# Softmax sums of added exponential tiles, and decodes of value weights dealt out over more groups

## The chip, the cores and the metric

The kernel runs on one core of a Trainium2 chip. The metric is the device time of one execution in microseconds (us). Engines are named as in the profile: PE is TensorE (matmuls; PEld is its weight load), DVE is VectorE, ACT is ScalarE, POOL is GpSimd, SP is SyncE, which issues the DMAs here. PE writes into PSUM, whose banks are handed out by a few pools.

## What is computed

Three stages, all in float32: an attention in which a query sees only the keys whose nearest cluster centroid is the same, and two feed-forward layers (called moe in the names, without routing).

```python
# attention: B=2, H=8, S=768, D=64; 16 centroids per head
mask   = q_assign[:, :, :, None] == k_assign[:, :, None, :]
scores = np.where(mask, (q @ k.T) / sqrt(D), -1e9)
attn   = np.exp(scores - scores.max(-1, keepdims=True))
attn   = attn / (attn.sum(-1, keepdims=True) + 1e-9)
x      = attn @ v                          # as 1536 tokens x 512
# layer 1: d_ff = 2048
h = x @ w_in;   x = (max(h, 0) + alpha * min(h, 0)) @ w_out
# layer 2: d_ff = 1536
xn = x / rms(x) * rms_g
x  = (silu(xn @ w_gate) * (xn @ w_val)) @ w_out2
```

The change touches the row sum `attn.sum(-1)` and the order in which weights of the layers are made ready.

## The kernel before, in words

**Attention.** Heads are taken in pairs, eight pairs in all. A pair has two phases, one for each half of its 768 queries, so there are 16 phases, numbered ph = 0 to 15. A phase has T = 6 key tiles of 128 keys, and every key tile has its own slot: phase ph covers the slots 6 ph to 6 ph + 5. In a slot, for each of the pair's two heads (e), `st_tile` (line 535) puts 128 keys x 384 queries of scores into one of three PSUM banks (two matmuls, L545 and L546), and ACT takes the exponential into a tile `p` of 128 x 2 x 384 (L547). Four such tiles exist, in turn. The maximum of each query has been found ahead, by `max_tile` (line 495): two matmuls into the one bank pair `ps_mx` (L503) and a reduction on DVE (L507), once per slot, nine slots before its use.

After every two key tiles, `pv_tiles` (line 549) runs in an even slot. It multiplies the two tiles with the values (L561, output of 64 partitions for each head) and then forms the row sums: matmuls with a matrix of ones (L566), each into 32 partitions of its own of a second bank `sm`, so that head e and tile y stand at partition 32 (2 e + y). The program's four matmuls of a call are eight records in the trace, since a float32 matmul takes two passes. A phase has three calls, for t0 = 0, 2 and 4, in the slots 6 ph + 2, + 4 and + 6. The first starts the accumulation in `sm`, the last ends it. `out_evac` copies both banks to SBUF, `out_sums` (L580) adds up the four partial sums of a query by a matmul, and `out_recip`, `out_bcast`, `out_mult` and `out_split` divide.

**What else runs in the slots.** Pairs are prepared ahead: cluster assignment of the pair's queries and keys, in small DVE steps, and the split of queries and keys into a high and a low part. The tables at the head of the file (PAIR for pairs 4 to 7) say in which slot, relative to the pair's first, each step stands, and in which order within the slot. `norm` are 14 DVE instructions on 128 x 24 (Newton steps of a reciprocal square root; lines 327 to 340), `hi` is a cast on ACT (L461) into a staging tile (`stage`), `lo` a subtraction on POOL (L467). DMAs on SP carry the staging tiles into the matmul operands (L471, L478 to L480); two staging tiles exist, so a pair's `hi` overwrites what the DMAs of the pair two before read. From slot 71 on, the first two halves of the layers' weights are decoded between the phases' work (EARLY). The pool of the preparation's tiles (`at_pre`) is closed at slot 80.

**Layers.** Weights come as 64-bit words and are decoded into a high and a low float32 half: on DVE (`word`, L784 and L786; `tail`, L789 and L790), with a cast on ACT (L797) and two subtractions and additions on POOL (L794, L795). A weight tile is decoded in two halves. Layer 1 has 8 groups of 256 hidden units, layer 2 has 6 (groups 8 to 13). For each group i and each of three blocks n of 512 tokens, `up(i, n)` makes 24 matmuls into two banks; ACT (L860, L861), DVE (L862), ACT (L869, the high part gh) and POOL (L870, the low part gl) follow for each. `down(i, n)` multiplies g with the output weights into ps_mx (y = 0) and ps_pv (y = 1), 12 matmuls each, and DVE adds each bank pair to x (L914). Layer 2 has a second up product with value weights `wv` (w_val).

**The order of the layers' work** is made by `plan` (line 960). It writes the sequence: up(p), then down of the step before p, so a down usually stands two of these slots behind its own up. At the end of layer 1, down(6, 2) is moved behind down(7, 0), so there up(7, 0), up(7, 1) and down(7, 0) follow each other. Decodes wait in the list `todo`, first in, first out. After the first half (y = 0) of every up or down one of them is placed, unless the slot is marked busy or the list is empty. At the end of the last up of group i, the up weights of group i + 2 are put on the list (two halves, or four with wv), at the end of its last down the down weights. The value weights of groups 8 and 9 (`split_v`) are put on it early: four groups ahead, that is at the ends of groups 4 and 5.

Of the kernel before, what the change touches and what calls it, by code (L numbers as in the profile page):

```python
# [13 lines left out]
ALU = mybir.AluOpType  # L14
# [8 lines left out]
    "load": ((-41, 6.1), (-41, 6.2), (-39, 6.1), (-38, 6.1)),  # L23
    "sq": ((-35, 4), (-34, 4)),
    "ss": ((-34, 5), (-33, 5)),
    "norm": tuple((-32 + n // 5, 5 + (n % 5) / 10) for n in range(14)),
    "hi": ((-32, 4), (-31, 4)),
    "lo": ((-28, 4.5), (-22, 4.5)),
    "sims": ((-30, 2.5), (-29, 1.7)),
# [50 lines left out]
    3: (11, 11, 12, 13, 14, 15),  # L80
}
DIRECT = 4
ASIDE = (1, 2, 3)
WARM = (6, 10, 1, 1, 3)
EARLY = (
# [93 lines left out]
class Attention:  # L179
    def __init__(self, base, core, ops, prep, tc, banks, qt, kt, qn, kn, vn, centroids, x1h, x1l, idf, idr):  # L180
        self.nc = tc.nc
        self.bk = banks
        self.qt, self.kt, self.qn, self.kn, self.vn = qt, kt, qn, kn, vn
        self.x1h, self.x1l, self.idf, self.idr = x1h, x1l, idf, idr
        self.NP, self.T, self.D = qn.shape[0], qn.shape[2], qn.shape[4]
        self.S = self.T * 128
        self.HS = self.S // 2
        self.NH = 2 * self.NP
        self.H, self.C = centroids.shape[:2]
        self.centroids = centroids  # L190
        self.scale = 1.0 / float(self.D) ** 0.5
        S, T, C = self.S, self.T, self.C

        def pool(ctx, name, bufs, **kw):
            return ctx.enter_context(tc.tile_pool(name=name, bufs=bufs, **kw))

        one = pool(core, "at_one", 1)
        self.v_p = pool(core, "at_vn", 2)
        self.p_p = pool(core, "at_p", 4)
        self.o_p = pool(core, "at_o", 2)  # L200
        self.x_p = pool(core, "at_x", 2)
        self.s_p = pool(core, "at_s", 2)
        pool(base, "at_pad", 1, side="right").tile([128, LINE - 8], F32, name="pad")
        stages = pool(base, "at_st0", 1, side="right"), pool(prep, "at_st1", 1, side="right")
        self.stages = [p.tile([128, 4, S], F32R, name=f"stage{i}") for i, p in enumerate(stages)]
        self.pre_p = pool(prep, "at_pre", 1, side="right")
        self.pre_p.tile([128, LINE // 4], F32, name="pad")
        ops = pool(ops, "at_ops", 1)
        self.op1 = [ops.tile([128, 2, S], F32R, name=f"op1_{i}") for i in range(4)]
        self.op2 = [ops.tile([82, 2, S], F32R, name=f"op2_{i}") for i in range(4)]  # L210
        self.cb = one.tile([128, self.H // 2, 2 * C], F32, name="cb")
        self.code = one.tile([128, C], F32, name="code")
        self.ohs = one.tile([128, 1], F32, name="ohs")
        self.rc0 = one.tile([128, 1], F32, name="rc0")
        self.mh = [one.tile([128, T // 2, 64], F32R, name=f"mh{i}") for i in range(2)]
        self.cb0 = one.tile([128, 2 * C], F32, name="cb0")
        self.sel = one.tile([128, LINE], F32, name="sel")[:, :2]
        for n in ("raw", "nat", "norm", "ss", "sims", "simc", "simp", "am", "oh", "oht", "pv", "P", "vnat",
                  "mx", "osb", "ssb", "sums", "rs", "R", "X"):
            setattr(self, n, {})  # L220
# [271 lines left out]
    def halves(self):  # L492
        return [(g, slice(g * self.HS, (g + 1) * self.HS)) for g in range(2)]
# [55 lines left out]
    def pv_tiles(self, u):  # L549


        nc, T = self.nc, self.T
        ph, t0 = divmod(2 * u, T)
        if t0 == 0:
            self.pv[ph] = self.bk.pv()
        ps, sm = self.pv[ph][:, 0, :self.HS], self.pv[ph][:, 1, :self.HS]
        P = [self.P.pop(2 * u + y) for y in range(2)]
        how = dict(start=t0 == 0, stop=t0 == T - 2)
        for y in range(2):
            for e in range(2):  # L560
                nc.tensor.matmul(ps[64 * e:64 * e + 64], lhsT=self.vnat[ph // 2][:, e, t0 + y], rhs=P[y][:, e],  # L561
                                 start=t0 + y == 0, stop=t0 + y == T - 1)
        for e in range(2):
            for y in range(2):
                r = 32 * (2 * e + y)
                nc.tensor.matmul(sm[r:r + 32], lhsT=self.ones[:, 0:32], rhs=P[y][:, e], **how)  # L566

    def out_evac(self, ph):
        nc = self.nc
# [118 lines left out]
class Moe:  # L688
# [271 lines left out]
    def plan(self):  # L960
# [10 lines left out]
        a, b = seq.index((self.down, (n1 - 2, NB - 1))), seq.index((self.down, (n1 - 1, 0)))  # L971
# [3 lines left out]
        tags = lambda i: ["wi", "wv"] if self.groups[i][0] else ["wi"]  # L975
        split_v = (n1, n1 + 1)
        halves = lambda i, ts: [(i, t, x) for t in ts for x in range(2)]
        out, dec, todo = [], [], []
        for i, t in ((1, "wi"), (0, "wo"), (1, "wo")):
            dec += halves(i, [t])  # L980
        pre = len(dec)
# [1 line left out]
        for fn, (i, n) in seq:  # L983
            last = n == NB - 1
            for y in range(2):
# [15 lines left out]
                        else:  # L1001
                            rms_at[self.up, *nxt[1], 1] = (self.rms_mul, n)
                if last and y and fn == self.up:
                    if i + 4 in split_v:
                        todo += halves(i + 4, ["wv"])
                    if i + 2 < NG:
                        todo += halves(i + 2, tags(i + 2)[:1] if i + 2 in split_v else tags(i + 2))
                if last and y and fn == self.down and i + 2 < NG:
                    todo += halves(i + 2, ["wo"])
                busy = (fn == self.down and (i == n1 - 1 or (i, n, y) == (n1 - 2, NB - 1, 1))  # L1010
# [144 lines left out]
```

## Time and profile before

| | us |
|---|---|
| median of three runs | 895.16 (894.52 to 896.11) |
| profiled execution, its own time | 896.74 |
| its span, first to last instruction | 895.0 |
| busy in the span: PE / DVE / POOL / ACT | 861.4 / 586.1 / 393.6 / 326.0 |
| mean granted clock of PE, share of 2.4 GHz | 0.985 |

Times in the profile are counted from the span's start. The attention's main loop runs from about 36 to 312 us, the layers from there to the end. A row of a timeline gives the start, the time, the engine, the line, the operation and its tiles; the bracket at its end is the engine's idle time before it and what ended it. "x8" means that eight instructions of the same kind are merged. Matmuls overlap, so starts of successive ones are closer than their durations.

### The profile page before, as it was taken

Reading aid. Unit: us, or ns where it says so; the run is one execution under the profiler, and the core shown is the slowest. Engines: PE = TensorE matmul, PEld = TensorE weight load, DVE = VectorE, ACT = ScalarE, POOL = GpSimd, SP = SyncE. Lnnn points to the kernel's source line nnn. Section 1 sums busy time; section 2 is a strip of 40 time slices with the busy share of each in tenths; the row PEclk is TensorE's granted clock in tenths of the full one; section 3 lists DMA queues with packets and bytes.
Section 4 is the critical chain, followed back from the end, with each engine's and each line's share of the span. In section 5 each row is a group of like instructions: output and inputs, shape, how many; then the busy total and the mean of one; then the engine's idle time right before and its main releaser. Section 6 shows DMA issues by size and latency. Waiting matters only on the chain.

```text
span 895.0 us, 11602 instructions
## 1 busy us (share of the span) xinstructions
PE 861.4 (96%) x4351; PEld 639.6 (71%) x4351; DVE 586.1 (65%) x906; ACT 326.0 (36%) x623; POOL 393.6 (44%) x349
## 2 busy tenths in 40 slices
PE   6898999999999999999999997999999999999998
PEld 4555565565555688888888875778888888888886
DVE  7765666565467546888778997887565465455422
ACT  4544465564445414333333334342212212222110
POOL 3651121121002516676657777433654554554511
PEclk9798999999999999999999998999999999999999
DMA  7768075265271201122212222000211211211012
GB/s 217 214 186 203 18 187 115 99 147 109 60 191 64 80 1 47 59 83 72 71 48 94 75 90 71 24 24 17 79 59 60 71 63 56 71 63 55 1 47 95
DMA packets 24279, 75.69 MB, mean 85 GB/s; under 512 B 3680, under 2 KB 4896, under 8 KB 24224
## 3 DMA queue, kind: packets, MB, share of 16 engines
q1 hardware_dynamic: 24224, 74.96, 29.1%
q8 instruction: 34, 0.56, 0.3%
q14 instruction: 21, 0.17, 0.1%
HBM read 51.46 MB, written 3.15 MB: 61 GB/s over the span
## 4 chain that ended last, share of the span: by engine, by line
PE 78%; DVE 10%; ACT 5%; issue 3%; POOL 1%; DMA 1%; SPq 1%; ACTq 0%; DVEq 0%
PE ps_st L807 26%; PE ps_mx L807 11%; PE ps_pv L807 10%; PE ps_pv L561 8%; PE ps_pr L807 5%; PE ps_pv L566 4%; PE ps_mx L503 4%; PE ps_st L545 3%; DVE dec_a L786 2%; PE ps_st L546 2%; PE ps_pr L594 2%; DVE x L914 1%; DVE dec_a L784 1%; ACT p L547 1%; ACT op L532 1%
## 5 line engine op out<-in xcount | busy, mean ns | idle before, releaser
L507 DVE TENSOR_REDUCE mx<-ps_mx 128x1 f32<-128x768 f32 x93 | 89.0, 957 | 85.2 <-PE ps_mx L503 84.7
L870 POOL TENSOR_TENSOR gl<-v,gh 128x512 fp32r<-128x512 f32 x68 | 93.7, 1378 | 110.3 <-ACT gh L869 108.5
L547 ACT ACTIVATE p<-ps_st 128x384 f32<-128x384 f32 x192 | 83.3, 496 | 57.7 <-PE ps_st L546 57.0
L611 POOL TENSOR_TENSOR x1l<-X,x1h 128x384 fp32r<-128x384 f32 x15 | 15.1, 1006 | 192.3 <-ACT x1h L608 192.3
L869 ACT CAST gh<-v 128x512 fp32r<-128x512 f32 x68 | 42.2, 621 | 134.4 <-DVE v L866 81.8
L866 DVE TENSOR_TENSOR v<-ps_st,t 128x512 f32<-128x512 f32 x36 | 24.9, 691 | 90.6 <-PE ps_st L807 90.6
L545 PE MATMUL ps_st<-op 128*128 128x384 f32 x192 | 71.4, 372 | 7.2 <-ACT p L547 7.2
L561 PE MATMUL ps_pv<-p,vnat 128*64 128x384 f32 x384 | 74.0, 507 | 0.0
L786 DVE SCALAR_TENSOR_TENSOR dec_a<-raw,dec_a 128x512 uint32<-128x512 uint32 x66 | 69.0, 1046 | 2.3
L862 DVE SCALAR_TENSOR_TENSOR v<-v,alpha,t 128x512 f32<-128x512 f32 x45 | 46.5, 1033 | 36.1 <-ACT v L861 36.1
L807 PE MATMUL ps_st<-x1h,stage 128*128 128x512 f32 x272 | 68.1, 391 | 0.0
L546 PE MATMUL ps_st<-op 82*128 82x384 f32 x192 | 66.1, 344 | 1.5 <-DMA op<-stage 1.5
L914 DVE TENSOR_TENSOR x<-ps_mx,x 128x1024 f32<-128x1024 f32 x36 | 43.8, 1218 | 32.6 <-PE ps_mx L807 32.6
L794 POOL TENSOR_TENSOR dec_a<-dec_a,woh 128x512 f32<-128x512 f32 x28 | 45.5, 1624 | 36.4 <-ACT woh L797 32.1
L503 PE MATMUL ps_mx<-op 80*128 80x384 f32 x186 | 54.7, 376 | 5.4 <-DVE mx L507 5.4
L807 PEld LDWEIGHTS ps_st<-x1h,stage 128*128 128x128 f32 x272 | 50.9, 188 | 11.0
L807 PE MATMUL ps_st<-x1h,wvh 128*128 128x512 f32 x144 | 57.1, 397 | 0.0
L807 PE MATMUL ps_st<-x1h,wvl 128*128 128x512 f32 x144 | 56.7, 394 | 0.0
L503 PEld LDWEIGHTS ps_mx<-op 80*128 80x128 f32 x186 | 31.5, 195 | 34.8 <-issue 15.6
L807 PE MATMUL ps_st<-x1h,wih 128*128 128x512 f32 x132 | 52.7, 399 | 0.1
L807 PE MATMUL ps_st<-x1h,wil 128*128 128x512 f32 x132 | 51.9, 393 | 0.0
L789 DVE TENSOR_SCALAR dec_e<-dec_a 128x512 uint32<-128x512 uint32 x66 | 49.5, 750 | 2.2
(250 smaller groups left out, 1989.3 us busy)
## 6 DMA issues: line engine op xcount, KB each, us to landing
raw<-in_moe_w_out_dram SPq DMA_DIRECT2D x28, 512.0 KB, 3.5
op<-stage SPq DMA_DIRECT2D x32, 384.0 KB, 5.7
raw<-in_moe_w_in_dram SPq DMA_DIRECT2D x15, 512.0 KB, 3.5
raw<-in_moe_w_val_dram SPq DMA_DIRECT2D x12, 512.0 KB, 3.4
raw<-in_moe_w_gate_dram SPq DMA_DIRECT2D x12, 512.0 KB, 3.4
op<-stage SPq DMA_DIRECT2D x16, 288.0 KB, 5.8
nat<-in_qn_dram SPq DMA_DIRECT2D x8, 384.0 KB, 5.1
nat<-in_kn_dram SPq DMA_DIRECT2D x8, 384.0 KB, 5.3
```

Of the source, the lines that this page charges most:

```text
L503: nc.tensor.matmul(ps[:, g, :self.HS], lhsT=o1[0:80, 0, t * 128:(t + 1) * 128], rhs=o1[0:80, 1, sl], start=True, stop=True)
L507: nc.vector.tensor_reduce(out=self.mx[ph][:, k:k + 1], in_=ps[:, :, :self.HS], op=ALU.max, axis=AX.XY)
L545: nc.tensor.matmul(ps, lhsT=o1[:, 1, ks], rhs=o1[:, 0, qs], start=True, stop=False)
L546: nc.tensor.matmul(ps, lhsT=o2[:, 1, ks], rhs=o2[:, 0, qs], start=False, stop=True)
L547: nc.scalar.activation(out=p[:, e], in_=ps, func=AF.Exp, scale=self.scale)
L561: nc.tensor.matmul(ps[64 * e:64 * e + 64], lhsT=self.vnat[ph // 2][:, e, t0 + y], rhs=P[y][:, e], start=t0 + y == 0, stop=t0 + y == T - 1)
L786: v.scalar_tensor_tensor(out=a, in0=top, scalar=0xC0000000, in1=a, op0=ALU.bitwise_and, op1=ALU.bitwise_or)
L789: v.tensor_scalar(out=e, in0=a, scalar1=0xFF800000, scalar2=None, op0=ALU.bitwise_and)
L807: self.nc.tensor.matmul(ps, lhsT=a, rhs=b, start=first and i == 0, stop=last and i == len(terms) - 1)
L862: nc.vector.scalar_tensor_tensor(out=v, in0=v, scalar=self.nalpha[:, a], in1=t, op0=ALU.mult, op1=ALU.add)
L870: nc.gpsimd.tensor_tensor(out=lo, in0=v, in1=f(hi), op=ALU.subtract)
L914: nc.vector.tensor_tensor(out=dst, in0=ps, in1=dst, op=ALU.add)
```

## The change

Three edits.

1. In phases 4 to 12 (`SUMMED`), the calls of `pv_tiles` with t0 = 0 and t0 = 2 issue no matmuls for the sums. Each adds its two exponential tiles on DVE into a tile of its own (`add0`, `add1`, 128 x 2 x 384, in the preparation's pool). The call with t0 = 4 then issues two rounds of the sums' matmuls: one over the two added tiles (it starts the accumulation), one over its own two tiles (it ends it).
2. The 14 `norm` steps of pairs 4 to 7 stand otherwise in the same three slots, -32, -31 and -30 before the pair: 1, 6 and 7 of them in place of 5, 5 and 4.
3. The decodes of the value weights of groups 8 and 9, four halves, are put on the list one at a time, at the ends of the last ups of groups 0, 1, 2 and 3, behind the up weights of group i + 2.

```diff
-    "norm": tuple((-32 + n // 5, 5 + (n % 5) / 10) for n in range(14)),
+    "norm": tuple((t, 5 + n / 100) for n, t in enumerate([-32] + [-31] * 6 + [-30] * 7)),
...
+SUMMED = range(4, 13)
...
+        self.adds = []
...
-        for e in range(2):
-            for y in range(2):
-                r = 32 * (2 * e + y)
-                nc.tensor.matmul(sm[r:r + 32], lhsT=self.ones[:, 0:32], rhs=P[y][:, e], **how)
+        if ph in SUMMED and t0 < T - 2:
+            a = self.pre([128, 2, self.HS], f"add{t0 // 2}")
+            self.adds.append(a)
+            nc.vector.tensor_tensor(out=a, in0=P[0], in1=P[1], op=ALU.add)
+            return
+        rounds = [self.adds, P] if ph in SUMMED else [P]
+        for x, q in enumerate(rounds):
+            if ph in SUMMED:
+                how = dict(start=x == 0, stop=x == 1)
+            for e in range(2):
+                for y in range(2):
+                    r = 32 * (2 * e + y)
+                    nc.tensor.matmul(sm[r:r + 32], lhsT=self.ones[:, 0:32], rhs=q[y][:, e], **how)
+        self.adds = []
...
-        out, dec, todo = [], [], []
+        out, dec, todo, split = [], [], [], [h for i in split_v for h in halves(i, ["wv"])]
...
                 if last and y and fn == self.up:
-                    if i + 4 in split_v:
-                        todo += halves(i + 4, ["wv"])
                     if i + 2 < NG:
                         todo += halves(i + 2, tags(i + 2)[:1] if i + 2 in split_v else tags(i + 2))
+                    todo += split[:1]
+                    split = split[1:]
```

Worked out by hand from this loop, the slots (one up or one down) that carry a decode change as follows. Before: six in a row from up(1, 2) to down(2, 0), then pairs with a free slot between them up to up(4, 0) and down(4, 0), then 14 in a row from down(4, 1) to up(7, 0). After: three from down(1, 0) to up(1, 1), 12 in a row from up(1, 2) to down(3, 0), five from down(3, 1) to down(4, 0), then pairs with a free slot between them up to up(7, 0). From group 8 on, both are the same.

## Rows read from the trace of the kernel before

**Rows 1.** Busy time by stretch: PE, PEld, DVE, ACT, POOL; PEclk; DMA share, GB/s.

```profile
100.00:300.00 200.00, 192.95 (x1311) 118.77 (x1308) 126.30 (x249) 100.27 (x228) 31.48 (x26) 1.00 0.47 117
300.00:540.00 240.00, 239.56 (x1080) 191.74 (x1080) 188.10 (x206) 89.79 (x162) 156.38 (x104) 1.00 0.19 64
```

**Rows 2.** Timeline of PE in slot 26: the call t0 = 0 of phase 4.

```profile
115.90 1.51 PE L561 MATMUL ps_pv<-p,vnat 128*64 128x384 f32 x8
...
116.28 0.14 PEld L561 LDWEIGHTS ps_pv<-p,vnat 128*64 128x64 f32 x2 [0.18 <-issue]
...
117.34 0.16 PEld L566 LDWEIGHTS ps_pv<-p,ones 128*32 128x32 f32 x8 [0.60 <-issue]
...
118.12 0.62 PE L503 MATMUL ps_mx<-op 80*128 80x384 f32 x2
```

**Rows 3.** Lines L467, L786 and L328 on DVE: durations in ns, least, median, greatest.

```profile
L467 DVE TENSOR_TENSOR stage<-raw,stage x2: 949/950/951, 16.1 to 16.9; 128x768 fp32r<-128x768 f32 x2
...
L786 DVE SCALAR_TENSOR_TENSOR dec_a<-raw,dec_a x66: 691/693/1674, 271.4 to 842.4; 128x512 uint32<-128x512 uint32 x66
...
L328 DVE SCALAR_TENSOR_TENSOR n_a<-n_a,n_y x9: 182/182/186, 123.5 to 194.6; 128x24 f32<-128x24 f32 x9
```

**Rows 4.** Timeline of DVE and PE in phase 12, around slots 77 and 78.

```profile
259.75 0.96 DVE L507 TENSOR_REDUCE mx<-ps_mx 128x1 f32<-128x768 f32 x1 [0.93 <-PE ps_mx L503]
...
261.17 0.52 PE L503 MATMUL ps_mx<-op 80*128 80x384 f32 x2
```

**Rows 5.** Timeline of ACT and PE in slot 29 (phase 4) and slot 41 (phase 6).

```profile
124.70 0.84 ACT L461 CAST stage<-raw 128x768 fp32r<-128x768 f32 x1 [3.08 <-DMA vnat<-in_vn_dram]
...
125.44 0.86 ACT L547 ACTIVATE p<-ps_st 128x384 f32<-128x384 f32 x2
...
126.06 0.37 PE L545 MATMUL ps_st<-op 128*128 128x384 f32 x1
...
158.31 0.83 ACT L461 CAST stage<-raw 128x768 fp32r<-128x768 f32 x1 [2.69 <-DMA vnat<-in_vn_dram]
...
160.05 0.34 PE L545 MATMUL ps_st<-op 128*128 128x384 f32 x1
```

**Rows 6.** Timeline of PE at down(7, 0), and one stretch of 2 us there.

```profile
546.97 0.39 PE L807 MATMUL ps_mx<-gh,woh 128*128 128x512 f32 x1
547.19 0.40 PE L807 MATMUL ps_mx<-gh,wol 128*128 128x512 f32 x1
...
552.06 0.80 PE L807 MATMUL ps_mx<-gh,woh 128*128 128x512 f32 x1 [4.46 <-ACT gh L869]
...
556.86 0.40 PE L807 MATMUL ps_pv<-gh,woh 128*128 128x512 f32 x1
...
550.00:552.00 2.00, 0.00 (x0) 0.00 (x0) 1.19 (x1) 0.74 (x3) 1.92 (x2) 0.50 0.56 168
```

**Rows 7.** Timeline within the run of 14 decodes: ACT, PE and DVE.

```profile
482.61 0.60 ACT L860 ACTIVATE t<-ps_st 128x512 f32<-128x512 f32 x1 [0.53 <-PE ps_st L807]
...
525.55 1.07 PE L807 MATMUL ps_st<-x1l,stage 128*128 128x512 f32 x4
...
530.76 0.59 ACT L860 ACTIVATE t<-ps_st 128x512 f32<-128x512 f32 x1
...
532.58 0.50 PE L807 MATMUL ps_pv<-gh,woh 128*128 128x512 f32 x1 [0.43 <-DVE x L914]
...
535.46 0.39 PE L807 MATMUL ps_st<-x1h,wih 128*128 128x512 f32 x1
...
543.48 1.22 DVE L914 TENSOR_TENSOR x<-ps_pv,x 128x1024 f32<-128x1024 f32 x1
```

**Rows 8.** Timeline around up(4, 0): the next matmul behind it on PE, POOL's gl.

```profile
440.91 0.40 PE L807 MATMUL ps_mx<-stage,woh 128*128 128x512 f32 x1
...
446.64 1.28 POOL L870 TENSOR_TENSOR gl<-v,gh 128x512 fp32r<-128x512 f32 x1
```

**Rows 9.** Busy time of one stretch in phase 2, columns as in rows 1.

```profile
82.00:90.00 8.00, 7.38 (x39) 4.31 (x37) 4.92 (x13) 3.04 (x6) 0.00 (x0) 0.57 0.54 194
```

## The prediction

> **What bounds the kernel now.** I read three views in order. First the busy time by stretch [rows 1]: between 100 and 300 us, the attention stage, TensorE (PE) is busy 193 of 200 us, and from 300 to 540 us, the first expert layer, 239.6 of 240. At these places a microsecond is won only by taking work from PE or by removing one of its few waits. Then PE's own instructions in one softmax slot [rows 2], to price the sums of the exponentials. Last the one large hole of PE behind 300 us, 547 to 552 us, with the queues of DVE, ScalarE (ACT) and POOL around it [rows 6]. PE waits there for an activation that DVE computed late. Behind the hole the granted clock is 0.50, its lower level of 1.2 GHz, where it was 1.00 while PE ran without a gap. So the change has two parts on PE's path, and one that only moves small DVE work (the norm steps).
>
> **Part A: sums of exponentials.** A phase has six key tiles, two per call of pv_tiles, and each call ends with one round of eight ones-matmuls (L566). A round costs PE from 117.34 to 118.12, 0.78 us, the start of the next line's matmuls included [rows 2]. In phases 4 to 12 the first two calls lose their round, the third gets a second one (over the two added tiles, ahead of the one over its own pair). So 2 x 0.78 goes and one round comes.
>
> The added round follows another of the same shape. Its nearest rows are the value matmuls just before: eight of them, two key tiles behind each other, take 115.90 to 117.34, 1.44 us or 0.72 per tile, and weight loads (116.28) run inside them. I take 0.72; the bounds are 0.64 (two steps of 0.32, the load of 116.28 and the gap before it) and 0.94 (a full 0.78, and 0.16 for loads that find nothing to hide behind). Net gain of a phase 1.56 - 0.72 = 0.84 us, of nine 7.6 us (bounds 5.6 to 8.3).
>
> The Trainium skill, page "TensorE: Matmul & The Clock Gate", section "Part 3: Packing small matmuls — row/col tiling", says that a weight load overlaps running matmuls only when the row groups differ. Here all loads cover the same 128 rows, so by it the second round would pay its loads in full, and the sum of part A would be 5.6, not 7.6. The trace goes the other way at the loads of 116.28, though those loads are 64 columns wide and the ones in question 32.
>
> **What DVE pays.** 18 additions of 128x768 with both inputs and output in SBUF. DVE did that shape twice, at 0.95 us [rows 3]; the upper bound is what a two-input DVE instruction takes when POOL runs beside it, 0.69 growing to 1.67. POOL is busy 31 of 200 us here [rows 1], so I take 0.95: 17 us of DVE in 150 us, on 126 of 200 busy [rows 1]. DVE has the time. Its order matters more: the addition stands ahead of the next maximum's reduction, and PE has one bank for maxima. In most slots the reduction still ends before PE asks for the bank; a shortened call (0.78 earlier) and the addition (0.95) together shift this by about 1.7 us.
>
> At one phase this does not fit. In phase 12 the first weights' decode shares the slots: before, the reduction of 259.75 ended at 260.7 and PE took the bank at 261.17 [rows 4]. Now PE would come 1.56 earlier, at 259.6, while the reduction comes no sooner: PE waits about 1.1 us, and 0.1 in the slot pair before. I price phase 12 at -1.2. The moved norm steps keep the other additions' slots free: of 14 instructions of 0.18 us [rows 3] four leave a slot with an addition for two without one. I price them at nothing, since DVE's idle time before the reductions covers them there; without it, 4 x 0.18 = 0.7 us in each of four pairs.
>
> **What DMA and ACT set.** In phases 4, 6 and 8 a cast on ACT (L461) overwrites a staging tile that DMAs of the previous pair still read. It starts when they land, at 124.70 after 3.08 us of idle ACT, and exponentials queue behind it (125.44) [rows 5]. The SP queue issues those DMAs back to back from the start of the phase, so their landing does not come earlier by what PE saves inside the phase. The fourth score tile needs the first one's exponential, one of the two that take 0.86: not before 125.9. Before it started at 126.06; PE could now be there 1.56 earlier, and gets only some 0.1 to 0.2. That loses 1.4 in phase 4. In phase 6 (cast 158.31 to 159.14, first exponential done 159.6, fourth tile at 160.05 before) PE is only 0.84 ahead, because the previous phase's longer last call lies behind the DMAs' start: it loses 0.4. Phase 8 has the same pattern, 0.6 at most. The smaller DVE waits of these phases fall into the same gaps. **Part A: 7.6 - 1.2 - 1.4 - 0.4 - 0.6 = 4.0 us**, between 2 and 7.6.
>
> **Part B: the decodes.** Before, four value-weight decodes are queued at groups 4 and 5, so that 14 slots in a row carry one each. DVE falls behind: the scores' first read came at once at 482.61 (ACT waited for PE), but at 530.76 for matmuls that ended at 526.6, eight slots later [rows 7]. So the lag grows 4.1 / 8 = 0.5 us per slot with a decode. Usually down(p) stands two slots behind up(p); at (7, 0) it stands one behind, and the lag becomes PE's wait. The two parts of that hole [rows 6]: 547.19 + 0.23 to 552.06 is 4.6 us of idle, and the 12 matmuls from 552.06 to 556.86 take 4.80 instead of 12 x 0.23 = 2.7 at full clock, 2.1 us. A bank wait of 0.43 at 532.58 comes from the same lag [rows 7]. Removable: 7.1 us.
>
> After, reading the schedule: groups 1 to 3 carry a run of 12 decodes in a row, then a gap, five, and from there two and a gap, up to (7, 0). That last pattern stood at (4, 0) before: the up group ended at 440.9, its last gl was ready at 446.64 + 1.28 = 447.9 [rows 8], 7.0 us later. The down group needs it one slot of 24 matmuls at 0.23 and five matmuls later, 5.5 + 1.1 = 6.6 us. So 0.4 us of wait remains at (7, 0), and the clock holds.
>
> The run of 12 brings its own lag, at its end the same as that of slots 12 and 13 before. There down's second bank was added at 543.48 + 1.2 = 544.7 for a down that ended when the next up began, 535.46: 9.2 us, and two slots later a down asks for that bank after 5.5 and 2.7 more, 8.2 [rows 6, 7]. So 1.0 us of new wait at down(3, 1), and 0.43 at down(3, 0) as at 532.58: 1.5 us, from 0 (the lag starts later) to 4.6 (as much as the hole of before). **Part B: 7.1 - 0.4 - 1.5 = 5.2 us**, between 0.5 and 7.1.
>
> The DMAs of the raw weights move with their decodes, three buffers ahead. Their queue, SP's, issues nothing else in that layer, and the DMA engines are busy 0.19 of it [rows 1], so I price that at nothing; if a load came late, its decode would wait on DVE and add to the same lag.
>
> **Sum.** 4.0 + 5.2 = 9.2 us. The profiled execution took 896.74 us, 895.0 in its span and 1.7 around it: 887.5. The median of the three runs shown is 895.16, 1.58 below it: **886.0 us**.
>
> **Rivals.**
> *All covers hold.* PE never waits for the additions, the cast or the run of 12: 7.6 + 7.1 - 0.4 = 14.3, so 880.9. For it: DVE is idle a third of the attention stage. Against it: the casts at 124.70 and 158.31, which PE hardly trails today. 20%.
> *The hole only moves.* The run of 12 stalls PE in group 3 as the run of 14 did: part B gives 0, 891.2. For it: the lag per slot is the same. Against: down stands two slots behind there. 12%.
> *The second round hides nothing.* It pays 0.78 and its loads' 0.16, the upper bound above: 9 x 0.22 = 2.0 us less, 888.0. For it: those loads stand in front of the first round today, after 0.60 of idle loader. Against: the loads at 116.28. 10%.
> *Part A does nothing.* Adding on DVE makes the maxima late in every phase, so that the matmuls saved are waited away: 890.0. 6%.
> *Slower: the clock.* From 82 to 90 us, where PE had waited shortly before (and idles for another 0.6 of the 8), the granted clock averaged 0.57 [rows 9], 0.43 x 8 = 3.4 us lost. New waits of 1 us stand at five places (phases 4, 6, 8, 12, group 3). If each brought one such fall, 17 us would go: 902.9; from the third fall on the change is slower. Against: most of the waits are shorter than 1 us, and stand alone. 6%.
> The Trainium skill, same page, section "HAM oscillation — how this bites in real kernels", says that gaps between bursts of matmuls bring the lower clock back, each anew; the rows at 80 to 90 us and at 552 us agree.
>
> **How the numbers follow.** The forecast has 46%. The range 880.5 to 891.5 takes in all but the clock rival and the forecast's own outer bounds. A difference under 0.2% (1.8 us) is about what a measurement of this kernel cannot tell from none. Every case but the clock's is faster by more, 0.94 together; I take 0.03 of that for both parts falling short at once: faster 0.91, within 0.03, slower 0.06.
>
> **What would show it.** Right: nine rounds of eight matmuls fewer from L566; 18 new DVE additions near 0.95 us; a summed phase 0.84 us shorter where no cast waits; ACT's cast in phases 4, 6, 8 still on DMA and the next score matmul waiting for an exponential; no hole near (7, 0) and a clock of 1.00 there; a small wait on ps_pv in group 3. Wrong: additions well above 1 us, PE waiting on L507 in every phase, or a low clock between 100 and 550 us.

## The result, and the profile after

| | before | after |
|---|---|---|
| median, runs beside each other (us) | 895.63 (894.52 to 897.06, 4 runs) | 887.08 (882.80 to 888.32, 4 runs) |
| profiled execution, its span (us) | 896.74, 895.0 | 886.97, 885.2 |
| busy PE / DVE / POOL / ACT (us) | 861.4 / 586.1 / 393.6 / 326.0 | 852.6 / 597.8 / 393.8 / 325.9 |
| mean granted clock | 0.985 | 0.988 |

The ratio is 0.9902, 95% interval 0.9875 to 0.9928: 8.6 us faster, against a forecast of 9.2. In the code after, the lines stand 3 further down, and 12 or 13 further behind the added ones: max matmul L506 and reduction L510 (503 and 507 before), scores L548 and L549, exponential L550, value matmul L564, addition L569, sums L578, copy of the sums L586, cast L464, layer matmul L820, addition to x L927.

First the busy time of the profiled execution after, by stretch (columns as in [rows 1]):

```profile
100.00:300.00 200.00, 190.29 (x1264) 120.34 (x1265) 143.35 (x271) 102.25 (x233) 36.01 (x29) 1.00 0.47 117
300.00:540.00 240.00, 238.82 (x1067) 191.47 (x1066) 192.81 (x211) 90.70 (x164) 158.75 (x105) 1.00 0.19 66
540.00:560.00 20.00, 20.00 (x91) 16.23 (x90) 14.02 (x26) 7.26 (x13) 7.37 (x6) 1.00 0.08 27
```

Against [rows 1] DVE has 17 us more in the attention, and the hole of [rows 6] is gone: PE works all 20 us around (7, 0), at clock 1.00. PE is *less* busy in the attention than before: it does less and waits a little more.

Then the lines of the addition and of its sums (durations in ns, least, median, greatest):

```profile
L569 DVE TENSOR_TENSOR add<-p x18: 916/932/948, 118.1 to 253.7; 128x768 f32<-128x768 f32 x18
...
L578 PE MATMUL ps_pv<-add,ones x72: 486/498/510, 128.8 to 259.0; 128*32 128x384 f32 x72
```

18 additions at 0.93 us (0.95 was taken); PE's matmuls fall from 4351 to 4279, the 9 x 8 expected.

**Phase by phase.** The copy of the sums on ACT ends every phase, and its start is in the trace to 0.01 us. From one copy to the next is the length of a phase. Before, phases 4 and 5:

```profile
112.71:130.28 17.57, 16.95 (x119) 10.52 (x120) 12.32 (x32) 10.86 (x24) 2.79 (x2) 1.00 0.90 228
130.28:146.71 16.43, 15.76 (x108) 9.53 (x107) 9.29 (x15) 7.18 (x19) 3.00 (x3) 1.00 0.17 32
```

The same phases after:

```profile
113.54:131.42 17.88, 16.24 (x111) 10.41 (x112) 13.77 (x34) 10.86 (x24) 2.80 (x2) 1.00 0.86 224
131.42:146.84 15.42, 14.76 (x100) 9.45 (x99) 10.81 (x17) 7.18 (x19) 3.00 (x3) 1.00 0.22 46
```

Phase 5 is 1.01 us shorter (16.43 - 15.42), all of it PE work. Phase 4 also lost 0.7 us of PE work, and is 0.31 *longer*: it waits. This table gives the difference for every phase, before minus the kernel named (us); the last six columns are the experiments below.

| phase | after | A alone | old norm | casts +1, +1 | casts +1, +2 | two additions | rounds apart |
|---|---|---|---|---|---|---|---|
| 4 | -0.31 | -0.74 | -2.27 | 0.98 | 0.98 | -1.59 | -2.65 |
| 5 | 1.01 | 1.00 | 1.00 | 0.25 | 1.00 | -0.10 | 0.86 |
| 6 | -0.07 | 0.50 | 0.11 | 0.93 | 0.91 | -1.02 | 0.42 |
| 7 | 0.99 | 0.99 | 0.99 | -1.31 | 1.00 | 0.13 | 0.87 |
| 8 | 0.27 | -0.18 | 0.12 | 0.93 | 0.94 | -0.99 | -0.58 |
| 9 | 0.97 | 0.97 | 0.99 | 0.25 | 0.98 | 0.11 | 0.84 |
| 10 | 0.91 | 0.91 | 0.92 | 0.92 | 0.91 | 0.64 | 0.79 |
| 11 | 0.60 | 0.60 | 0.61 | 0.60 | 0.60 | -0.39 | 0.46 |
| 12 | 0.22 | 0.22 | 0.24 | 0.24 | 0.22 | -3.37 | 0.09 |
| 4 to 12 | 4.59 | 4.27 | 2.71 | 3.79 | 7.54 | -6.58 | 1.10 |

So the 9.8 us between the two spans are: 4.59 in phases 4 to 12; 6.01 from the last copy to the last addition to x, the layers; and -0.83 up to the end of phase 3, where the two kernels differ only in the order of the norm steps of slots 16 to 18. Of this 0.71 stands ahead of the first copy, in the start-up and phase 0, which the change does not touch.

### The profile page after: what moved, and what is told of

The parts are those of the page before. It is cut to its first block, busy times and chain, and to the rows that moved or that the text cites. A ratio compares the mean times of both kernels' runs of the same rounds, so it can differ in the third digit from the quotient of the medians.

```text
span 885.2 us, 11463 instructions
## 1 busy us (share of the span) xinstructions
PE 852.6 (96%) x4279; PEld 637.5 (72%) x4279; DVE 597.8 (68%) x924; ACT 325.9 (37%) x623; POOL 393.8 (44%) x349
## 4 chain that ended last, share of the span: by engine, by line
PE 77%; DVE 11%; ACT 5%; issue 3%; DMA 2%; POOL 1%; SPq 1%; ACTq 0%; DVEq 0%
PE ps_st L820 27%; PE ps_mx L820 11%; PE ps_pv L820 11%; PE ps_pv L564 7%; PE ps_pr L820 5%; PE ps_mx L506 4%; PE ps_pv L578 3%; PE ps_st L548 3%; DVE mx L510 2%; DVE dec_a L799 2%; PE ps_st L549 2%; DVE x L927 2%; ACT p L550 1%; DMA op<-stage 1%; PE ps_pr L607 1%
## 5 line engine op out<-in xcount | busy, mean ns | idle before, releaser
L510 DVE TENSOR_REDUCE mx<-ps_mx 128x1 f32<-128x768 f32 x93 | 88.8, 955 | 67.9 <-PE ps_mx L506 67.7
L550 ACT ACTIVATE p<-ps_st 128x384 f32<-128x384 f32 x192 | 83.3, 496 | 51.6 <-PE ps_st L549 51.0
L548 PE MATMUL ps_st<-op 128*128 128x384 f32 x192 | 71.7, 373 | 9.4 <-ACT p L550 9.4
L564 PE MATMUL ps_pv<-p,vnat 128*64 128x384 f32 x384 | 74.3, 509 | 0.0
L820 PE MATMUL ps_st<-x1h,stage 128*128 128x512 f32 x272 | 68.1, 391 | 0.0
L549 PE MATMUL ps_st<-op 82*128 82x384 f32 x192 | 66.1, 344 | 1.1 <-DMA op<-stage 1.1
L927 DVE TENSOR_TENSOR x<-ps_mx,x 128x1024 f32<-128x1024 f32 x36 | 43.9, 1218 | 32.4 <-PE ps_mx L820 32.4
L506 PE MATMUL ps_mx<-op 80*128 80x384 f32 x186 | 55.0, 377 | 5.9 <-DVE mx L510 5.8
L820 PEld LDWEIGHTS ps_st<-x1h,stage 128*128 128x128 f32 x272 | 50.9, 188 | 11.0
L820 PE MATMUL ps_st<-x1h,wvh 128*128 128x512 f32 x144 | 57.1, 396 | 0.0
L506 PEld LDWEIGHTS ps_mx<-op 80*128 80x128 f32 x186 | 31.1, 194 | 35.8 <-DVE mx L510 12.0
L820 PE MATMUL ps_st<-x1h,wvl 128*128 128x512 f32 x144 | 56.7, 394 | 0.0
L820 PE MATMUL ps_st<-x1h,wih 128*128 128x512 f32 x132 | 52.5, 398 | 0.0
L820 PE MATMUL ps_st<-x1h,wil 128*128 128x512 f32 x132 | 51.9, 393 | 0.0
L548 PEld LDWEIGHTS ps_st<-op 128*128 128x128 f32 x192 | 37.2, 194 | 20.4 <-ACT p L550 19.4
```

The costliest lines, as they stand in the source:

```text
L506: nc.tensor.matmul(ps[:, g, :self.HS], lhsT=o1[0:80, 0, t * 128:(t + 1) * 128], rhs=o1[0:80, 1, sl], start=True, stop=True)
L510: nc.vector.tensor_reduce(out=self.mx[ph][:, k:k + 1], in_=ps[:, :, :self.HS], op=ALU.max, axis=AX.XY)
L548: nc.tensor.matmul(ps, lhsT=o1[:, 1, ks], rhs=o1[:, 0, qs], start=True, stop=False)
L549: nc.tensor.matmul(ps, lhsT=o2[:, 1, ks], rhs=o2[:, 0, qs], start=False, stop=True)
L550: nc.scalar.activation(out=p[:, e], in_=ps, func=AF.Exp, scale=self.scale)
L820: self.nc.tensor.matmul(ps, lhsT=a, rhs=b, start=first and i == 0, stop=last and i == len(terms) - 1)
```

## The experiments

Ten kernels ran. Where a time differs by less than 1%, the phases say more than the medians.

**1. Part A alone: the decodes as before.**

```diff
-        out, dec, todo, split = [], [], [], [h for i in split_v for h in halves(i, ["wv"])]
+        out, dec, todo = [], [], []
...
+                    if i + 4 in split_v:
+                        todo += halves(i + 4, ["wv"])
...
-                    todo += split[:1]
-                    split = split[1:]
```

> Part A without part B: the added sums and the moved norm steps, with the decodes queued as before. Theory (the two parts are independent; A is worth 4.6 us between the ends of phases 3 and 12, B is the hole at (7, 0)): the copy of the sums at the end of phase 12 stands 4.6 us closer to that of phase 3 than before, within 0.4; the hole of 4.6 us near (7, 0) and the half clock behind it are still there; time 4.6 below the kernel before, ratio 0.995. Rival (A and B share something, for example DVE's lag is carried from one to the other): the hole shrinks or grows by over 1 us, and the time is below 0.993 or above 0.997.

891.38 us, ratio 0.9954 (0.9934 to 0.9974). 4.27 in phases 4 to 12, 0.09 in the layers. Its waits of PE from 312 to 560 us (us in total, times, longest):

```profile
PE ps_mx L820 <- ACT gh L882: 4.5, 1, 4.5
PE ps_pv L820 <- DVE x L927: 0.4, 1, 0.4
```

The hole is there in full. The theory holds.

**2. Part B alone: the kernel before with the decodes dealt out** (the reverse edit in the kernel before).

> Part B without part A: the decodes dealt out over four groups, sums as before. Theory: no hole near (7, 0), clock 1.00 there, waits of about 1.1 us on ps_pv in group 3, 6.0 us gained between the start of layer 1 and its end, nothing in the attention stage; ratio 0.9933. Rival (part A brought some of the gain in the layer): 4 us or less, ratio above 0.995.

889.92 us, ratio 0.9932 (0.9907 to 0.9958). No phase from 4 to 12 differs by more than 0.08; the layers gain 6.15, where the seven traces with these layers give 6.01 to 6.17. The hole is gone, and ps_pv waits 1.1 us, in 2 waits. The two parts add up, within their intervals: 0.46% and 0.68% against 0.98% together. What fell short of the theory's "nothing in the attention stage" is phase 2, 2.94 us shorter with the same instructions (see the clock below).

**3. The norm steps back at 5, 5 and 4.**

```diff
-    "norm": tuple((t, 5 + n / 100) for n, t in enumerate([-32] + [-31] * 6 + [-30] * 7)),
+    "norm": tuple((-32 + n // 5, 5 + (n % 5) / 10) for n in range(14)),
```

> The changed kernel with the norm steps of pairs 4 to 7 back at 5, 5 and 4 a slot. Theory (DVE's idle time before the reductions covers them): every phase as in the changed kernel within 0.2 us, the same time within 0.5 us. Rival (an addition and five norm steps in one slot make the maximum late): up to 0.7 us in each of four pairs, 2.8 us slower, with waits of the maxima's matmuls on DVE's reduction in phases 1, 3, 5 and 7 after the pair's start three ahead.

885.75 us, ratio 0.9889 (0.9861 to 0.9917), not to be told from the changed kernel. Every phase of the table but 4, 6 and 8 agrees within 0.02. Phase 4 lost 2.27, but not to a reduction: PE waited 1.38 there for an exponential behind the cast, and the clock then fell (0.65 on average from 125 to 128 us). So no gain of the moved norm steps shows in the time. But in phase 8 the rival's wait is there. With the steps back, five of them stand between the addition and the reduction, which ends at 192.80:

```profile
190.03 0.94 DVE L569 TENSOR_TENSOR add<-p 128x768 f32<-128x768 f32 x1
...
191.85 0.95 DVE L510 TENSOR_REDUCE mx<-ps_mx 128x1 f32<-128x768 f32 x1
...
192.85 0.62 PE L506 MATMUL ps_mx<-op 80*128 80x384 f32 x2 [0.35 <-DVE mx L510]
```

In the changed kernel one step stands there, and the reduction ends 0.88 before PE comes, which had waited for the cast:

```profile
189.88 0.94 DVE L569 TENSOR_TENSOR add<-p 128x768 f32<-128x768 f32 x1
...
190.83 0.95 DVE L510 TENSOR_REDUCE mx<-ps_mx 128x1 f32<-128x768 f32 x1
...
192.66 0.52 PE L506 MATMUL ps_mx<-op 80*128 80x384 f32 x2
```

So it is mostly the wait for the cast that covers the old order in phases 4, 6 and 8, and not DVE's idle time. The order moves the reduction's end by 0.87 (2.77 or 1.90 behind the start of the addition). Without the cast's wait (experiment 5) the margin there is only 0.22, so by estimate the old order would cost about 0.65 in each of these phases; no run shows it.

**4. The hi casts of pairs 4 to 7 one slot later.** What phase 4 waits for, in the changed kernel, on ACT:

```profile
125.20 0.83 ACT L464 CAST stage<-raw 128x768 fp32r<-128x768 f32 x1 [3.54 <-DMA vnat<-in_vn_dram]
125.94 0.86 ACT L550 ACTIVATE p<-ps_st 128x384 f32<-128x384 f32 x2
```

and on PE:

```profile
126.47 0.44 PE L548 MATMUL ps_st<-op 128*128 128x384 f32 x1 [1.01 <-ACT p L550]
```

This is the chain of the prediction: DMA, cast, exponential, fourth score tile. The bracket names a load of v, but that is inferred. On SP's queue the last DMA that reads the staging tile stands just ahead of it:

```profile
119.19 1.90 SPq L483 DMA_DIRECT2D op<-stage  x1
121.19 1.38 SPq L361 DMA_DIRECT2D vnat<-in_vn_dram  x1
```

The first landed 5.8 us after its start, at 125.0, just before the cast; the load landed after 4.5 us, at 125.7, when the cast was running. If this chain is the cause, moving the cast alone must free all three phases.

```diff
-    "hi": ((-32, 4), (-31, 4)),
+    "hi": ((-31, 4), (-30, 4)),
```

> The changed kernel with both hi casts of pairs 4 to 7 one slot (about 5 us) later. Theory (the cast that waits for DMAs holds ACT, and the exponentials behind it hold the score tiles): the cast finds its tile free, phases 4, 6 and 8 come to the 0.97 us gained by the undisturbed phases, from -0.31, -0.07 and 0.27: 3.0 us faster than the changed kernel, ratio to the kernel before 0.987. Rival 1 (the maxima's bank behind the additions holds PE in those phases as well): under 1 us of it comes. Rival 2 (the casts now delay another exponential, or the operands' DMAs start later and arrive late): no gain, or up to 1 us slower.

885.49 us, ratio 0.9886 (0.9862 to 0.9911). Phases 4, 6 and 8 gain 0.98, 0.93 and 0.93, as the theory said to 0.05. But phases 5, 7 and 9 (and 3, by 0.54) lost, as the first half of rival 2 said (the casts delay another exponential). ACT around the start of phase 7:

```profile
161.10 0.49 ACT L400 ACTIVATE simc<-ps_pr 128x384 f32<-128x384 f32 x1 [2.39 <-PE ps_pr L395]
161.49 0.47 ACT L586 COPY ssb<-ps_pv 128x384 f32<-128x384 f32 x1
161.85 0.50 ACT L586 COPY osb<-ps_pv 128x384 f32<-128x384 f32 x1
162.22 0.86 ACT L464 CAST stage<-raw 128x768 fp32r<-128x768 f32 x1
162.95 0.53 ACT L621 CAST x1h<-X 128x384 fp32r<-128x384 f32 x1
163.36 1.71 ACT L550 ACTIVATE p<-ps_st 128x384 f32<-128x384 f32 x4
```

The second cast now stands in the slot in which ACT already makes four other copies, and the exponentials come after all five. PE, and then its clock (last number but two of the stretch 165 to 168):

```profile
163.93 0.45 PE L548 MATMUL ps_st<-op 128*128 128x384 f32 x1 [0.95 <-ACT p L550]
...
165.00:168.00 3.00, 3.00 (x13) 1.16 (x12) 2.59 (x6) 0.08 (x1) 1.33 (x1) 0.56 0.00 0
```

In phases 5 and 9 the wait cost 0.7 to 0.8; in phase 7 a clock of 0.56, near the lower level of 1.2 GHz, followed, and 2.3 us went.

**5. The second cast one slot further**, past the copies.

```diff
-    "hi": ((-32, 4), (-31, 4)),
+    "hi": ((-31, 4), (-29, 4)),
```

> The changed kernel with the hi casts of pairs 4 to 7 one and two slots later, so that none stands in the slot in which ACT also copies the sums out. Theory (the landing of the previous pairs' DMAs sets phases 4, 6 and 8, and the copy's slot was what cost phases 5, 7 and 9 in the kernel with both casts one slot later): phases 4, 6 and 8 gain 0.95 as there, phases 5, 7 and 9 gain 0.97 again as in the changed kernel; together about 3 us over the changed kernel, at 884. Rival (any later place of the cast meets some exponential): phases 5, 7 and 9 stay at 0.25 or less, and the sum is 1 us or less.

880.03 us, ratio 0.9840 (0.9816 to 0.9863). All six phases at 0.91 to 1.00; phases 4 to 12 give 7.54 instead of 4.59, the 3 us expected. The cast finds its tile free, and the exponentials do not wait (ACT in phase 4):

```profile
121.41 0.58 ACT L444 ACTIVATE oht<-ps_pr,ohs 128x384 fp32r<-128x384 f32 x1
121.88 0.84 ACT L464 CAST stage<-raw 128x768 fp32r<-128x768 f32 x1
122.60 0.89 ACT L550 ACTIVATE p<-ps_st 128x384 f32<-128x384 f32 x2
```

So the DMAs' landing, through the cast on ACT, took 3 us of what the additions saved.

**6. The dealing at groups 0, 2, 3 and 4.**

```diff
-                    todo += split[:1]
-                    split = split[1:]
+                    if i in (0, 2, 3, 4):
+                        todo += split[:1]
+                        split = split[1:]
```

> The changed kernel with the value weights' halves put on the list at the last ups of groups 0, 2, 3 and 4, so that the longest run of slots with a decode is 6 instead of 12 (runs of 3, 6, 5, 5, 5, then 2, 2, 2). Theory (DVE's lag grows 0.5 us per slot of a run and costs PE from about the tenth on): no wait on ps_pv in group 3, none elsewhere, no hole at (7, 0); 1.1 us faster than the changed kernel in the first layer. Rival 1 (a run of 5 with one gap carries its lag over): the waits only move to groups 4 to 6, same time. Rival 2 (with the fourth half nearer to the end, DVE is late at (7, 0)): part of the hole of 4.6 us and of the low clock is back, 1 to 5 us slower.

882.29 us, ratio 0.9872 (0.9836 to 0.9908). No wait of PE is listed from 312 to 560 us. From 400 to 440 us, in this kernel:

```profile
400.00:440.00 40.00, 40.00 (x175) 32.55 (x174) 36.27 (x39) 15.06 (x27) 30.10 (x21) 1.00 0.25 80
```

and in the changed one:

```profile
400.00:440.00 40.00, 38.87 (x167) 31.02 (x166) 36.74 (x41) 14.98 (x27) 30.03 (x21) 1.00 0.24 82
```

DVE is about as busy; it only never has 12 decodes in a row. The layers gain 8.21 over the kernel before, 2.0 to 2.2 more than with the change's order, where the theory took 1.1 from the waits as listed. The list is too low. One of the two waits, PE in the changed kernel:

```profile
429.10 0.63 PE L820 MATMUL ps_mx<-gl,woh 128*128 128x512 f32 x2
430.49 0.50 PE L820 MATMUL ps_pv<-gh,woh 128*128 128x512 f32 x1 [0.77 <-DVE x L927]
430.83 0.40 PE L820 MATMUL ps_pv<-gh,wol 128*128 128x512 f32 x1
```

Matmuls start 0.23 apart when nothing is late. Two from 429.10, then the one of 430.49: the matmul after that should start at 429.79, and starts at 430.83, 1.04 later; the bracket says 0.77. The other wait is 0.62 by its starts (two from 417.36, the second behind them at 418.67), where the bracket says 0.36. Together 1.66. A third wait for this bank, behind the run of five decodes, is not listed at all: two matmuls from 463.13, the second behind them at 464.15 and not at 463.82, 0.33 late, just after DVE's addition to x ended at 463.77. The three together are 2.0, which is what this order gains. At (7, 0) 0.13 is left in both kernels (in the changed one two from 545.09, the next at 545.68).

**7. Each addition issued twice.**

```diff
             nc.vector.tensor_tensor(out=a, in0=P[0], in1=P[1], op=ALU.add)
+            nc.vector.tensor_tensor(out=a, in0=P[0], in1=P[1], op=ALU.add)
```

> The changed kernel with each of the 18 additions issued twice. Theory (DVE has time; in the phases without decodes the reductions end before PE asks for the maxima's bank): the clean phases 5, 7, 9 and 10 keep their gain of 0.9 to 1.0, and phases 11 and 12, where decodes share the slots, lose another 0.5 to 0.95 for each addition that stands ahead of a late reduction, 1 to 3 us in all. Rival (the additions are just hidden and no more): every phase loses up to 0.93 a call, 1.9 a phase, and the change's gain in the attention is gone.

896.01 us, ratio 1.0005 (0.9986 to 1.0025): the whole gain of part A and more is gone, and the theory falls. Of the 1.0 of phases 5, 7 and 9 nothing or 0.1 is left; phases 10 and 11 lose 0.3 and 1.0 against the change, phase 12 3.6. In phases 4 and 12 the clock averages 0.91, by estimate 1.7 and 1.8 us of each (0.09 of 19.2 and 19.8). DVE in phase 5 (L569 and L570 are the two additions):

```profile
140.52 0.95 DVE L569 TENSOR_TENSOR add<-p 128x768 f32<-128x768 f32 x1
141.50 0.96 DVE L570 TENSOR_TENSOR add<-p 128x768 f32<-128x768 f32 x1
...
142.85 0.95 DVE L510 TENSOR_REDUCE mx<-ps_mx 128x1 f32<-128x768 f32 x1
```

and the matmul that wants the bank of that reduction:

```profile
143.85 0.62 PE L506 MATMUL ps_mx<-op 80*128 80x384 f32 x2 [0.47 <-DVE mx L510]
```

In the changed kernel the same reduction ends at 143.03, and PE comes at 143.38, a margin of 0.35:

```profile
142.08 0.95 DVE L510 TENSOR_REDUCE mx<-ps_mx 128x1 f32<-128x768 f32 x1
...
143.38 0.52 PE L506 MATMUL ps_mx<-op 80*128 80x384 f32 x2
```

DVE is idle over a quarter of the attention (143 of 200 us busy), but a second instruction of 0.95 does not fit in front of this reduction. Behind the second addition of phase 10 the margin was 0.54, and behind the first ones of phases 5, 7, 9 and 10 0.84 to 1.08; of these four the loss is smallest in phase 10. For L510 alone PE waited 8.2 us, in 11 waits. The rival ("just hidden and no more") is right in direction; a clean phase lost 0.9 to 1.1 and not 1.9, since the first addition's margin mostly held.

**8. The added tiles' round ahead of the value matmuls.**

```diff
+        if self.adds and t0 == T - 2:
+            sums(0, self.adds, how)
+            self.adds = []
         for y in range(2):
             for e in range(2):
                 nc.tensor.matmul(ps[64 * e:64 * e + 64], lhsT=self.vnat
...
-        rounds = [self.adds, P] if ph in SUMMED else [P]
...
+        sums(1, P, how)
```

(`sums` issues one round; it is the change's loop over e and y, made a function.)

> The changed kernel with the round over the added tiles ahead of the third call's value matmuls, so that it no longer stands directly in front of the other round. Theory (the second round is cheap, about 0.6 in place of 0.78, because its weight loads run inside the round before it): the clean phases 5, 7, 9 gain 0.78 or less instead of 0.97, some 1.2 to 2 us slower over nine phases. Rival (a round costs the same wherever it stands): the same within 0.3 us. Rival 2 (the moved round waits for the addition on DVE): a wait on DVE's addition shows in front of it, and more is lost.

886.65 us, ratio 0.9910 (0.9881 to 0.9940). The two rounds in the changed kernel, phase 5, and the matmul behind them:

```profile
145.27 0.85 PE L578 MATMUL ps_pv<-add,ones 128*32 128x384 f32 x8
145.94 0.83 PE L578 MATMUL ps_pv<-p,ones 128*32 128x384 f32 x8
146.70 0.62 PE L506 MATMUL ps_mx<-op 80*128 80x384 f32 x2
```

and apart (L568 the rounds, L575 the value matmuls between them):

```profile
145.20 0.85 PE L568 MATMUL ps_pv<-add,ones 128*32 128x384 f32 x8
145.98 1.51 PE L575 MATMUL ps_pv<-p,vnat 128*64 128x384 f32 x8
147.42 0.85 PE L568 MATMUL ps_pv<-p,ones 128*32 128x384 f32 x8
148.20 0.62 PE L506 MATMUL ps_mx<-op 80*128 80x384 f32 x2
```

Together 1.43 us, apart 0.78 each. So the second round costs 0.65 behind its like, and 0.13 more elsewhere: phases 5, 7, 9 to 12 give 0.86, 0.87, 0.84, 0.79, 0.46, 0.09, that is 0.12 to 0.15 less than in the changed kernel. The theory's direction is right, its size (0.2 a phase and more) was too large; the first rival (a round costs the same wherever it stands) falls. Of rival 2 there is no wait on an addition. Phase 4 lost 2.65 to the cast (a wait of 1.65) and a low clock behind it.

**9. Both moves together** (experiments 5 and 6).

> Both gains at once: the hi casts one and two slots later, and the value weights' halves at groups 0, 2, 3 and 4. Theory (they lie in different stages and share nothing): phases 4, 6 and 8 gain 0.9 to 1.0, the first layer is without PE waits, 4.1 us less than the changed kernel between the end of phase 3 and the end of the first layer; ratio to the kernel before 0.983, apart from what the clock does in phase 2. Rival (the casts' gain brings DVE or the raw loads of the layers under pressure): one of the two gains shrinks by over 0.5 us.

877.47 us, ratio 0.9804 (0.9777 to 0.9831). Phases 4 to 12 give 7.55, the layers 8.21: both gains whole.

**10. And the first decodes out of the additions' way.** What phases 11 and 12 lack in every kernel above are reductions behind an addition *and* a decode step. One of them, in phase 12 of the changed kernel (L802 and L803 are the decode step):

```profile
253.72 0.95 DVE L569 TENSOR_TENSOR add<-p 128x768 f32<-128x768 f32 x1
254.59 0.42 DVE L802 TENSOR_SCALAR raw<-nat 128x512 uint32<-128x512 uint32 x1
255.04 0.69 DVE L803 SCALAR_TENSOR_TENSOR raw<-raw 128x512 f32<-128x512 uint32 x1
255.65 0.95 DVE L510 TENSOR_REDUCE mx<-ps_mx 128x1 f32<-128x768 f32 x1
...
256.65 0.62 PE L506 MATMUL ps_mx<-op 80*128 80x384 f32 x2 [0.37 <-DVE mx L510]
```

```diff
-    (71, -1),
+    (71, 9),
...
-    (76, 9),
-    (77, 2.55),
-    (78, 9),
+    (77, 9),
+    (78, 2.55),
+    (79, 9),
```

> The kernel with both moves, and in addition the first weights' decode steps in phases 11 and 12 put where no reduction waits behind an addition and a decode: the first word step behind slot 71's reduction instead of ahead of it, the second tail step in slot 77 instead of 76 (its later steps one slot on). Theory (what phases 11 and 12 lack, 0.4 and 0.75 us, is the reduction that stands behind an addition and a decode step): phase 11 gains 0.3 to 0.4 more, phase 12 another 0.4, 0.7 us in all. Rival (the steps only delay another reduction): phases 11 and 12 stay at 0.60 and 0.22, or phase 13 loses what they gain.

876.29 us, ratio 0.9803 (0.9770 to 0.9836). Phase 11 gives 1.01 and phase 12 0.85, from 0.60 and 0.22, 1.0 us where the theory took 0.7, and phase 13 loses nothing: phases 4 to 12 are now worth 8.56. Its phases 11 and 12:

```profile
219.93:235.35 15.42, 14.80 (x98) 9.54 (x99) 10.50 (x17) 7.18 (x18) 1.00 (x1) 1.00 0.21 43
235.35:250.94 15.59, 14.96 (x98) 9.49 (x99) 11.59 (x19) 8.15 (x20) 1.00 (x1) 1.00 0.95 234
```

This beats both kernels: about 1% below the changed one (0.9803 over 0.9902). Against experiment 9 the medians do not tell it apart; the phases do, by 1.0 us.

## Why the prediction was right

Time, sign and both mechanisms held; the terms were off by up to 1.1 us, and partly against each other. That the sum of spans comes within 0.6 us is in part luck: parts A and B gave 10.6 and not 9.2, and the start-up, which no term covers, took 0.83 back.

| term | predicted | measured | from |
|---|---|---|---|
| a clean phase (5, 7, 9, 10) | 0.84 | 0.91 to 1.01 | phases after |
| second round | 0.72 | 0.65 | experiment 8 |
| phases 11 and 12 short of clean | 1.2, all in 12 | 0.37 + 0.75 = 1.1 | phases after; 10 |
| casts, phases 4 / 6 / 8 | 1.4 / 0.4 / 0.6 | 1.3 / 1.0 / 0.7 | phases after; 5 |
| norm steps | 0 | 0 | experiments 3, 5 |
| part A | 4.0 | 4.59 | phases after |
| removable in the layers | 7.1 | 8.2 | experiment 6 |
| new waits of the run of 12 | 1.5 | 1.66 | starts of matmuls |
| new wait behind the run of five | 0 | 0.33 | starts of matmuls |
| left at (7, 0) | 0.4 | 0.13 | starts of matmuls |
| part B | 5.2 | 6.0 | layers |
| sum, spans | 9.2 | 9.8 | 4.59 + 6.01 - 0.83 |

**The second round.** Its price was taken from the value matmuls, 0.72, and is 0.65. In the trace the loads of the second round start at 145.62 and 145.94, within the matmuls of the first (145.27 to 146.12, an end that is modelled) and of its own. Phases 5, 7 and 9 gain 0.06 to 0.10 more than two rounds of 0.78 less 0.65 give; with the rounds apart it is 0.06 to 0.09 more than 0.78 as well, so this lies outside the rounds. It was not placed. With it a clean phase lies above the prediction's upper bound (1.56 - 0.64 = 0.92).

The Trainium skill, page "TensorE: Matmul & The Clock Gate", section "Part 3: Packing small matmuls — row/col tiling", has a sentence by which loads overlap running matmuls only across row groups; the same section also names a background weight buffer as a second way. By that sentence alone a clean phase would have gained an estimated 0.62 (1.56 - 0.94). The trace does not agree with it: a clean phase gained 0.91 to 1.01.

**The casts.** The mechanism was right, with one slip: the DMAs are those of the pair two before (it has the same staging tile), not of the previous pair. The sum was 2.4 against 3.0. In this trace phase 6 was the mis-sized one: "PE is only 0.84 ahead" there, yet it lost 1.04. But the term has no one value, since the landing itself moves from run to run. The same attention code lacks 1.71, 0.47 and 1.15 in phases 4, 6 and 8 of experiment 1, and 1.01, 0.77 and 0.25 in experiment 6, sums of 3.3 and 2.0, so one trace does not tell a wrong price from this spread. Phase 4's wait was 1.01 in the changed kernel, 1.45 in experiment 1, 1.38 in 3, 0.73 in 6, and 1.65 in 8, with the same queue.

**The norm steps.** At their new places they cost nothing, as priced: with the casts moved, phases 4, 6 and 8 gain 0.91 to 0.98 (experiment 5). That moving them was worth nothing in experiment 3 is due to the wait for the cast, which covers the old places as well. The prediction's 0.7 concerns three pairs and not four, since pair 4's steps stand in slots 16 to 18, ahead of the first addition.

**Phase 12.** "PE waits about 1.1 us, and 0.1 in the slot pair before" was right in sum, but a third of it stands in phase 11, at the first word step ahead of slot 71's reduction, which the prediction did not look at. Experiment 10 gives back 0.41 and 0.63 by moving these steps.

**The decodes.** The half-clock matmuls and the hole were read correctly, but the removable waits were 8.2, not 7.1. By starts, the bank wait of 532.58 [rows 7] is 0.71, not 0.43 (two matmuls from 531.51, the second behind them at 532.91 and not at 532.20), and another of 0.36 is not listed (four from 542.89, the second behind them at 544.40 and not at 544.04). Some 0.4 in the layers of before stay without a place.

**The rivals.** *The hole only moves* fell: 12 decodes in a row cost 1.7, and 14 in a row had cost 7.4 by starts (4.64 of hole, 2.07 of half clock, 0.71 at the bank), where (7, 0) has only one slot of distance between up and down. *All covers hold* fell in the changed kernel, at the cast, at phases 11 and 12 and in group 3. But its conditions can be made: with the three moved away (experiment 10) the phases and the layers give 8.56 + 8.21 = 16.8 us, more than that rival's 14.3. *Part A does nothing* fell by 0.35 us of margin, as experiment 7 shows; its 6% looked small for so thin a margin. *The clock* did not strike in the changed kernel's new waits, where it stayed at 1.00 in phases 4 to 12 and in group 3. Such falls are real: the clock fell after listed waits of 0.95, 1.38 and 1.65 us in experiments 4, 3 and 8, which cost about 1.6 us each time (phase 7 of experiment 4: -1.31 against 0.25 in phases 5 and 9, which have the same wait and kept 1.00), and after 0.68 and 1.31 in experiment 7. So that most waits are shorter than 1 us, as the prediction argued, is no protection by itself.

## What to carry to other kernels

Work taken off the bounding engine and given to another counted here by the *margin* in front of the next thing that engine must deliver, not by its idle share: 0.35 us beside a DVE that idles over a quarter of the time. An in-order engine that waits for a DMA before overwriting a buffer holds everything behind it; here that wait was the largest new one when the phases got shorter, and a later slot that is free of other work on that engine cured it. Of several due items, spread the ones on the late engine so that no run of them ends just where a consumer stands one slot behind.

## What was not expected

**The same code, three lengths.** Phase 2 is the same instruction for instruction in the kernel before and in experiment 2. From 82 to 90 us, in experiment 2, against [rows 9]:

```profile
82.00:90.00 8.00, 7.38 (x54) 4.82 (x55) 6.84 (x21) 4.78 (x11) 0.00 (x0) 1.00 0.55 189
```

Both have the same two waits on DVE shortly before and at its start, 1.05 and 0.62 us. Before, the clock averages 0.57; in experiment 2 it stays at 1.00, and phase 2 is 2.94 us shorter. Over the twelve traces, phase 2 took three lengths: that of before (within 0.1; four traces), 1.4 less (three), and 2.9 less (five). The changed kernel and experiments 1, 6, 7 and 8, which do the same there, show all three. This is as much as most terms of the sum, and single times of one kernel spread by more (882.80 to 888.32 for the changed one). What decides it the traces do not show. Nor does the length of the wait alone decide it: in phase 4, PE lost no clock after 1.01 (the changed kernel) and 1.45 us (experiment 1), but did after 1.38 (experiment 3).

**Idle in brackets is a lower bound.** A matmul's record ends later than the start of the next one when PE runs freely (0.39 long, 0.23 apart), so idle time counted from the end of a record leaves out part of each wait: 0.77 for 1.04, 0.36 for 0.62, nothing for 0.33. The Trainium skill, page "Perfetto Trace Analysis", section "Tensor Engine Instruction (MATMUL, LD_WEIGHTS)", says that these ends are estimated from the instruction's size; the starts agree with it, and for a wait of PE the distance of starts is the measure.
